# A queue that narrows the float64 weights of the first MLP ahead of their use, and GpSimd for all weight remainders of its first token block

## The chip, the cores and the metric

The kernel runs on one core of one Trainium2 chip. The metric is device time in microseconds (us). The kernel before takes 721.33 us, the median of three runs between 718.95 and 722.62.

## The reference

What is computed is an attention layer with two MLPs behind it, all in float32 accuracy; the weights come as float64.

```python
scores = scale * q @ k.T + bias            # 2 batches, 8 heads, 768 positions, 64 wide
keep = (pos_k < n_global) | (0 <= rel < n_local)
x = softmax(where(keep, scores, -1e9)) @ v # -> 1536 tokens x 512
h = x @ w_in                               # 512 -> 2048
x = (h * cos(h)) @ w_out                   # 2048 -> 512
g = x @ w_gate; val = x @ w_val            # 512 -> 1536, twice
out = (silu(g) * val) @ w_out              # 1536 -> 512
```

## The kernel before, in words

**Tiling.** Tokens go in 12 attention tiles of 128 and in three MLP blocks of 512 (`BLOCKS`). A weight matrix goes in tiles of 128 x 512; the first MLP has 16 of `w1i` and 16 of `w1o`, `NF1` = 16. A float64 weight tile is 512 KB in memory.

**From float64 to two tiles.** `fetch` (L167) loads such a tile into one of the three buffers `st` (L174, on SP's queue). The function that it returns, `narrow`, makes float32 of it on VectorE by three instructions, L183, L186 and L193. The float32 tile `w` stays for the whole kernel. For every use it is split anew: ScalarE makes the rounded main part (L206), and VectorE or GpSimd the remainder (L210). A letter in `WIE` (for `w1i`) and in `WOE` (for `w1o`) says which of the two does the remainder of step n: D for VectorE, G for GpSimd. Every matrix product runs as three TensorE products of main parts and remainders.

**Prologue.** The attention tiles 0 to 3 and the loads for them come first. Its loop (L1007) has 12 windows w. A window issues the scores of one pair of heads' groups (`scores_pair`), the split and the DMA transposes of the window before (`split_p`, L862 and L864), and the products with v two windows later (`pv`, L890). `begin` (L365), called in window 5, fetches `w1i` 0 and 1 and `w1o` 0, narrows the first two and splits the first.

**Steps of the first MLP.** Then come 48 steps s, 16 for each token block (L378 for the first 32). A step has 12 matmuls for h (L274) and 12 for y of two steps before (L350), and a chain of elementwise work for g * cos between them (L300 to L338). In the 16 steps of the first block a step also fetches `w1i` s+2 and `w1o` s+1 (`get`) and, at its end, narrows `w1i` s+2 and `w1o` s (`use`). The attention tiles 4 to 11 are spread over these steps by `BASES`. From step 32 on, and in the second MLP, the order is written out by hand.

**What sets the order.** Until step 32 a planner at compile time orders each engine's instructions from the order in which the code issues them, its own estimates of times, and the buffers; on the chip each engine then runs its list strictly in order. SP's queue is such a list, too: a fetch that waits until a buffer `st` is free holds up the loads of q, k and v and the transposes behind it.

Of the kernel before, what the change touches and what calls it, by code (L numbers as in the profile page):

```python
# [15 lines left out]
I32 = mybir.dt.int32  # L16
# [6 lines left out]
P = 128  # L23
B, H, S, D = 2, 8, 768, 64
NTOK = B * S
DM = H * D
# [19 lines left out]
VSE = "GDDGGGGGGDDD"  # L46
VLE = "DGGGDDDGDDGD"
PLE = "DGGGGGGGDGGGGGGGDGDGGGGGGGGGGDDDDDGDDGDDDDDGDGDG"
WIE = "GGGGGDGGGGGDGGGGDGDGGGDGGDDGDGDGDDDDDDDDDDDDDDDD"
WOE = "GDGDDGDGDDDDGGGGGDDGGGGGGGGDGGGGDDDDDDDDDDDDDDDD"  # L50
SQE = "----DAAAAAAA"
VHE = "DDDDDDDDGDDD"
GKE = "DAAAAADAAAAA"
# [3 lines left out]
VBE = 6  # L57
HB = 5
HE = 6
GVE = "DMMDDDDDDMDM"  # L60
M1E = "GDDGGDG"
ACE = "DDDDDDDD"
# [7 lines left out]
def attention_moe_moe2_kernel(  # L70
# [15 lines left out]
    NF1 = w1i.shape[0]  # L86
# [7 lines left out]
    xy_p = ctx.enter_context(tc.tile_pool(name="xy", bufs=1))  # L94
    wr_p = ctx.enter_context(tc.tile_pool(name="wr", bufs=2 * NF1))
    ws_p = ctx.enter_context(tc.tile_pool(name="ws", bufs=2))
    st_p = ctx.enter_context(tc.tile_pool(name="st", bufs=3))

    n32 = const.tile([P, 2, 2], I32, name="n32")
    for j, src in enumerate((n_global, n_local)):  # L100
# [66 lines left out]
    def fetch(src, j, pool=wr_p, tag="w"):  # L167

        if not wide:
            w = pool.tile([P, DM], F32, tag=tag, name="w")  # L170
            nc.sync.dma_start(out=w, in_=src[j])
            return lambda half=None: w
        t = st_p.tile([P, DM, 2], I32, tag="st", name="st")
        nc.sync.dma_start(out=t, in_=src[j].bitcast(I32).rearrange("p (n w) -> p n w", w=2))  # L174

        part = []

        def narrow(half=None):
            hi, lo = t[:, :, 1], t[:, :, 0]
            if not part:  # L180
                w = pool.tile([P, DM], I32, tag=tag, name="w")
                part.append(w)
                nc.vector.tensor_scalar(  # L183
                    w, hi, 0x07FFFFFF, 3, op0=ALU.bitwise_and, op1=ALU.logical_shift_left
                )
                nc.vector.scalar_tensor_tensor(  # L186
                    out=w, in0=hi, scalar=-(1 << 30), in1=w,
                    op0=ALU.bitwise_and, op1=ALU.bitwise_or,
                )
            w = part[0]  # L190
            if half == 0:
                return None
            nc.vector.scalar_tensor_tensor(  # L193
                out=w, in0=lo, scalar=29, in1=w,
                op0=ALU.logical_shift_right, op1=ALU.bitwise_or,
            )
            return w.bitcast(F32)

        return narrow

    def eng(which, n):
        return nc.vector if n < len(which) and which[n] == "D" else nc.gpsimd
# [20 lines left out]
    def x_split(i, xT):  # L223
        cols = slice(i * P, (i + 1) * P)
        nc.scalar.copy(out=xh[:, :, cols], in_=xT)  # L225
        nc.vector.tensor_tensor(  # L226
            out=xl[:, :, cols], in0=xT, in1=f32(xh[:, :, cols]), op=ALU.subtract
        )
# [16 lines left out]

    def first_mlp(c1, before, steps, last_block):
        w_in, w_out = {}, {}
        got = {}
        todo = [(b, j) for b in range(len(BLOCKS)) for j in range(NF1)]
        nsteps = len(todo)  # L250
        hp = c1.enter_context(tc.tile_pool(name="hp", bufs=2, space=PSUM))
        wis, wos, hps, hs, fs, gs, ys = {}, {}, {}, {}, {}, {}, {}

        def get(nm, j):
            if j < NF1 and (nm, j) not in got:
                got[nm, j] = fetch(w1i if nm == "i" else w1o, j)

        def use(nm, d, j):
            if j < NF1 and j not in d:
                d[j] = got.pop((nm, j))()  # L260

        def prep_in(s):
            if s < nsteps and s not in wis:
# [99 lines left out]
                    )  # L363

        def begin():  # L365
            get("i", 0)
            get("i", 1)
            get("o", 0)
            use("i", w_in, 0)
            use("i", w_in, 1)  # L370
            prep_in(0)

        before(hp, begin, prep_in, h_early)
        ch_p = c1.enter_context(tc.tile_pool(name="ch", bufs=2))
        g_p = c1.enter_context(tc.tile_pool(name="g", bufs=2))
        yp = c1.enter_context(tc.tile_pool(name="yp", bufs=4, space=PSUM))
        last = nsteps - NF1
        for s in range(last):  # L378
            early, late = steps.get(s, ((), ()))
            if s < NF1:  # L380
                get("i", s + 2)
                get("o", s + 1)
            ps = h_mm(s)
            if s >= 2:
                y_mm(s - 2)
            prep_in(s + 1)
            if s >= 1:
                chain_b(s - 1)
            for th in early:
                th()  # L390
            if s >= 1:
                chain_c(s - 1)
                chain_d(s - 1)
            if s < NF1:
                use("i", w_in, s + 2)
                use("o", w_out, s)
            prep_out(s - 1)
            chain_a(s, ps)
            for th in late:
                th()  # L400
# [186 lines left out]
    def windowed_path():  # L587
# [7 lines left out]
        with ExitStack() as ca:  # L595
# [373 lines left out]
                s: tuple([th for _, th in w] for w in e) for s, e in sched.items()  # L969
            }  # L970

            def prologue(hp, begin, prep_in, h_early):
                with (
                    tc.tile_pool(name="pps", bufs=2, space=PSUM, side="right") as pps,
                    tc.tile_pool(name="pv0", bufs=1, side="right") as pv0,
# [31 lines left out]
                    for w in range(NW + LAG + 2):  # L1007
                        if w < NW:
                            i, pp = pairs[w]
# [22 lines left out]
                        if w >= 1 and w - 1 < NW:  # L1032
                            i, pp = pairs[w - 1]
                            for p in (2 * pp, 2 * pp + 1):
                                pools["p"] = (pph, ph_p)[pp]
                                split_p(i, p, eng(PLE, 4 * i + p), nc.scalar.copy)
                        if w == HB:
                            begin()
                        if w == HB + 1:
# [21 lines left out]
    def general_path():  # L1061
        half = TB // 2 * P
        with ExitStack() as cg:
# [19 lines left out]
            for b in range(B):  # L1083
# [6 lines left out]
                for t in range(TB):  # L1090
# [62 lines left out]
                    xn = wk.tile([P, DM], F32, tag="xn", name="gxn")  # L1153
                    nc.vector.tensor_copy(out=xn, in_=x)
                    x_split(i, x_turn(xn, ps_x, "xT"))
        moe(lambda hp, begin, *_: begin(), {}, lambda: None)

    with tc.If(windowed != 0) as branch:
# [45 lines left out]
```

## Time and profile before

| | us |
|---|---|
| median of 3 runs | 721.33 |
| lowest, highest run | 718.95, 722.62 |
| the profiled execution | 719.88 |
| its span, first to last instruction | 718.1 |
| busy in the span: TensorE, VectorE, ScalarE, GpSimd | 668.2, 484.5, 390.0, 112.3 |

All times inside the kernel below come from the profiled execution. PE is TensorE, DVE is VectorE, ACT is ScalarE, POOL is GpSimd, SP the queue that issues the DMAs. The position of a step is read from the count of its matmuls at L274: step 0 ends near 72 us, step 10 starts near 155 us, step 16 near 207 us.

### The profile page before, as it was taken

What the parts mean: (1) busy time and instruction counts of PE and PEld (TensorE: products, weight loads), DVE (VectorE), ACT (ScalarE), POOL (GpSimd) and SP (SyncE); (2) the same over time, 40 slices, a digit from 0 to 9 for tenths busy, and PEclk for the clock granted to TensorE, in tenths of its full rate; (3) what the DMA queues carried; (4) which work ended last, traced back from release to release, by engine and by line L of the source; (5) the groups of instructions that cost most, each with busy time, mean ns of one, the idle gap of its engine ahead of it and who ended that gap; (6) DMA issues with size and microseconds to landing.
All of it is one profiled execution on the core that took longest, in us unless ns stands there. A gap on an engine that the chain in (4) does not pass through costs nothing.

```text
span 718.1 us, 9055 instructions
## 1 busy us (share of the span) xinstructions
PE 668.2 (93%) x3276; PEld 525.9 (73%) x3276; DVE 484.5 (67%) x885; ACT 390.0 (54%) x816; POOL 112.3 (16%) x108
## 2 busy tenths in 40 slices
PE   4767986997998999999999999999999999999996
PEld 2446764775776777787888888888888888888884
DVE  3897899799988565747999779887544443434441
ACT  4675757578497887766666643333343333333331
POOL 2663323423222332420000000000000000000000
PEclk9776899798999999999999999999999999999998
DMA  6799656657552222300322224532100000100001
GB/s 216 184 205 230 166 138 206 137 152 193 147 117 60 40 40 45 60 1 30 112 93 89 88 59 135 158 118 88 38 22 0 1 1 0 59 0 1 1 0 63
DMA packets 69508, 62.73 MB, mean 87 GB/s; under 512 B 48880, under 2 KB 55024, under 8 KB 69456
## 3 DMA queue, kind: packets, MB, share of 16 engines
q1 hardware_dynamic: 69456, 62.08, 31.8%
q8 instruction: 27, 0.44, 0.3%
q14 instruction: 25, 0.20, 0.1%
HBM read 47.19 MB, written 3.15 MB: 70 GB/s over the span
## 4 chain that ended last, share of the span: by engine, by line
PE 77%; DVE 11%; DMA 6%; ACT 3%; issue 1%; POOL 0%; SPq 0%; DVEq 0%; ACTq 0%; POOLq 0%
PE h L274 15%; PE v L492 14%; PE g L492 14%; PE o L528 14%; PE y L350 14%; PE s L753 3%; DMA st<-w1i 2%; DVE w L186 2%; PE x L890 1%; PE s L777 1%; DVE w L193 1%; DMA pt<-ph 1%; DVE w L183 1%; DMA v<-v 1%; DVE h L328 1%
## 5 line engine op out<-in xcount | busy, mean ns | idle before, releaser
L210 DVE TENSOR_TENSOR ws<-w,ws 128x512 fp32r<-128x512 f32 x161 | 111.2, 711 | 93.8 <-ACT ws L206 93.6
L350 PE MATMUL y<-g,ws 128*128 128x512 f32 x576 | 145.1, 397 | 12.6 <-ACT g L332 11.0
L274 PE MATMUL h<-xh,ws 128*128 128x512 f32 (+1 forms) x392 | 137.4, 411 | 2.7 <-ACT xh L225 2.5
L350 PEld LDWEIGHTS y<-g,ws 128*128 128x128 f32 x576 | 108.6, 191 | 39.1 <-ACT g L332 12.9
L206 ACT CAST ws<-w 128x512 fp32r<-128x512 f32 x204 | 121.8, 616 | 21.8 <-DVE w L193 16.8
L528 PE MATMUL o<-ws,a 128*128 128x512 f32 x432 | 104.7, 391 | 0.0
L492 PE MATMUL v<-xh,ws 128*128 128x512 f32 x288 | 96.3, 395 | 0.0
L274 PEld LDWEIGHTS h<-xh,ws 128*128 128x128 f32 x392 | 77.9, 201 | 24.1 <-ACT xh L225 3.2
L492 PE MATMUL g<-xh,ws 128*128 128x512 f32 x288 | 94.7, 390 | 0.0
L528 PEld LDWEIGHTS o<-ws,a 128*128 128x128 f32 x432 | 81.1, 188 | 18.4
L274 PE MATMUL h<-xl,ws 128*128 128x512 f32 (+1 forms) x196 | 79.7, 407 | 3.3 <-DVE xl L226 3.3
L210 POOL TENSOR_TENSOR ws<-w,ws 128x512 fp32r<-128x512 f32 x43 | 58.6, 1363 | 134.6 <-ACT ws L206 126.6
L504 ACT ACTIVATE sl<-g 128x512 f32<-128x512 f32 x36 | 21.5, 598 | 97.5 <-PE g L492 97.5
L492 PEld LDWEIGHTS v<-xh,ws 128*128 128x128 f32 x288 | 54.2, 188 | 12.7
L492 PEld LDWEIGHTS g<-xh,ws 128*128 128x128 f32 x288 | 54.1, 188 | 11.2
L514 ACT CAST a<-sl 128x512 fp32r<-128x512 f32 x36 | 22.4, 623 | 72.5 <-DVE sl L510 72.5
L492 PE MATMUL v<-xl,ws 128*128 128x512 f32 x144 | 56.9, 395 | 0.0
L492 PE MATMUL g<-xl,ws 128*128 128x512 f32 x144 | 56.0, 389 | 0.0
L186 DVE SCALAR_TENSOR_TENSOR w<-st,w 128x512 int32<-128x512 int32 x68 | 51.0, 760 | 1.2
L193 DVE SCALAR_TENSOR_TENSOR w<-st,w 128x512 int32<-128x512 int32 x68 | 50.2, 746 | 0.8
L300 ACT ACTIVATE k<-h 128x512 int32<-128x512 f32 x48 | 28.5, 594 | 39.3 <-PE h L274 39.2
L274 PEld LDWEIGHTS h<-xl,ws 128*128 128x128 f32 x196 | 39.4, 201 | 12.4 <-DVE xl L226 4.0
(109 smaller groups left out, 822.2 us busy)
## 6 DMA issues: line engine op xcount, KB each, us to landing
st<-w1i SPq DMA_DIRECT2D x16, 512.0 KB, 3.9
st<-w1o SPq DMA_DIRECT2D x16, 512.0 KB, 4.4
st<-w2g SPq DMA_DIRECT2D x12, 512.0 KB, 3.8
st<-w2v SPq DMA_DIRECT2D x12, 512.0 KB, 3.7
st<-w2o SPq DMA_DIRECT2D x12, 512.0 KB, 3.8
vr<-v SPq DMA_DIRECT2D x16, 256.0 KB, 3.8
kr<-kT SPq DMA_DIRECT2D x12, 256.0 KB, 3.8
qr<-qT SPq DMA_DIRECT2D x12, 256.0 KB, 3.7
```

The source lines that it names most:

```text
L186: nc.vector.scalar_tensor_tensor(out=w, in0=hi, scalar=-(1 << 30), in1=w, op0=ALU.bitwise_and, op1=ALU.bitwise_or,)
L193: nc.vector.scalar_tensor_tensor(out=w, in0=lo, scalar=29, in1=w, op0=ALU.logical_shift_right, op1=ALU.bitwise_or,)
L206: nc.scalar.copy(out=s[:, 0, :], in_=w)
L210: e.tensor_tensor(out=s[:, 1, :], in0=w, in1=f32(s[:, 0, :]), op=ALU.subtract)
L274: nc.tensor.matmul(hps[s][:, c0:c1], lhsT=wis[s][:, a, k * P:(k + 1) * P], rhs=xx[:, k, t0 + c0:t0 + c1], start=(k == 0 and a == 0 and xx ...
L300: nc.scalar.activation(out=k[:, :n], in_=ps[:, :n], func=AF.Copy, scale=INV2PI)
L350: nc.tensor.matmul(ys[b][m][:, :n], lhsT=w[:, a, m * P:(m + 1) * P], rhs=g[:, c, :n], start=(j == 0 and a == 0 and c == 0), stop=(j == NF1 ...
L492: nc.tensor.matmul(ps[:, :n], lhsT=w[:, a, k * P:(k + 1) * P], rhs=xx[:, k, t0:t0 + n], start=(k == 0 and a == 0 and xx is xh), stop=(k == ...
L504: nc.scalar.activation(out=sl[:, :n], in_=ps_.pop(("g", s))[:, :n], func=AF.Silu)
L514: nc.scalar.copy(out=a[:, 0, :n], in_=sl[:, :n])
L528: nc.tensor.matmul(os_[b][m], lhsT=a[:, c, m * P:(m + 1) * P], rhs=w[:, d, :], start=(j == 0 and c == 0 and d == 0), stop=(j == NF2 - 1 an ...
L753: nc.tensor.matmul(o, lhsT=qr[r, i % 3, c, :], rhs=k, start=True, stop=True)
```

## The change

It does two things. First, the fetches and the narrowing of the first MLP's 32 weight tiles no longer follow the steps. A list `order` holds them in the order of use; `fetch_next` fetches the next one; `conv1` narrows the oldest one fetched and fetches the next. Three fetches are issued at the very start, ahead of the branch and so ahead of the loads of k, q and v for the tiles 1 and on. In the prologue's windows `conv1` is called `CV[w]` times, 13 times in all in the windows 0 to 10; each step of the first block calls it twice, and `need(s)` calls it more often only where a tile would be missing. The three buffers `st` become one tile with three slots, used in turn. Second, ten letters D in the first 16 places of `WIE` and `WOE` become G: 5 and 11 in `WIE`; 1, 3, 4, 6, 8, 9, 10 and 11 in `WOE`.

```diff
-WIE = "GGGGGDGGGGGDGGGGDGDGGGDGGDDGDGDGDDDDDDDDDDDDDDDD"
-WOE = "GDGDDGDGDDDDGGGGGDDGGGGGGGGDGGGGDDDDDDDDDDDDDDDD"
+WIE = "GGGGGGGGGGGGGGGGDGDGGGDGGDDGDGDGDDDDDDDDDDDDDDDD"
+WOE = "GGGGGGGGGGGGGGGGGDDGGGGGGGGDGGGGDDDDDDDDDDDDDDDD"
+CV = (2, 2, 1, 1, 1, 1, 1, 1, 1, 1, 1)
...
-    st_p = ctx.enter_context(tc.tile_pool(name="st", bufs=3))
+    st_p = ctx.enter_context(tc.tile_pool(name="st", bufs=1))
+    st = st_p.tile([P, 3, DM, 2], I32, name="st")
+    taken = [0]
...
-        t = st_p.tile([P, DM, 2], I32, tag="st", name="st")
+        t = st[:, taken[0] % 3]
+        taken[0] += 1
...
+    order = [t for j in range(NF1 + 2) for t in (("i", j), ("o", j - 2)) if 0 <= t[1] < NF1]
+    fetched = []
+    def fetch_next():
+        if order:
+            nm, j = order.pop(0)
+            fetched.append(((nm, j), fetch(w1i if nm == "i" else w1o, j)))
+    for _ in range(3):
+        fetch_next()
...
+        def conv1():
+            if fetched:
+                (nm, j), fn = fetched.pop(0)
+                (w_in if nm == "i" else w_out)[j] = fn()
+                fetch_next()
+        def need(s):
+            while (s + 2 < NF1 and s + 2 not in w_in) or (s < NF1 and s not in w_out):
+                conv1()
...
         def begin():
-            get("i", 0)
-            get("i", 1)
-            get("o", 0)
-            use("i", w_in, 0)
-            use("i", w_in, 1)
+            while 1 not in w_in:
+                conv1()
             prep_in(0)
...
             if s < NF1:
-                get("i", s + 2)
-                get("o", s + 1)
...
             if s < NF1:
-                use("i", w_in, s + 2)
-                use("o", w_out, s)
+                conv1()
+                conv1()
+                need(s)
...
+                        for _ in range(CV[w] if w < len(CV) else 0):
+                            conv1()
                         if w == HB:
                             begin()
```

## Rows read from the trace of the kernel before

**Rows 1.** The page's part 2: busy tenths in 40 slices of 18 us.

```profile
PE   4767986997998999999999999999999999999996
DVE  3897899799988565747999779887544443434441
```

**Rows 2.** Busy time by stretch: PE, PEld, DVE, ACT, POOL, granted clock, DMA share, GB/s.

```profile
12.00:72.00 60.00, 43.24 (x305) 27.85 (x305) 44.06 (x74) 38.22 (x120) 28.67 (x24) 0.77 0.88 222
72.00:155.00 83.00, 73.04 (x359) 54.24 (x359) 73.36 (x151) 57.07 (x124) 29.13 (x22) 0.88 0.61 166
155.00:207.00 52.00, 47.47 (x252) 36.03 (x251) 49.69 (x103) 36.32 (x85) 14.39 (x12) 0.93 0.59 162
207.00:330.00 123.00, 121.03 (x686) 94.26 (x685) 78.60 (x161) 96.55 (x198) 36.19 (x28) 1.00 0.21 38
```

**Rows 3.** The chain that ended last: start us, us, what.

```profile
7.46 5.53 DMA v<-v
22.18 4.94 DMA vr<-v
...
61.41 3.58 DMA pt<-ph
...
104.73 3.96 DMA st<-w1i
108.69 0.02 issue
108.72 0.76 DVE w L183 x2
```

**Rows 4.** The prologue's first loads: two SP issues, then two stretches (columns of Rows 2).

```profile
2.39 0.60 SPq L115 DMA_DIRECT2D qr<-qT  x1
6.20 0.56 SPq L110 DMA_DIRECT2D kr<-kT  x1
...
8.00:12.00 4.00, 1.97 (x11) 1.26 (x10) 2.94 (x10) 1.22 (x4) 1.50 (x2) 1.00 0.86 268
12.00:20.00 8.00, 5.71 (x17) 2.69 (x19) 1.03 (x4) 5.88 (x23) 0.01 (x1) 1.00 0.75 280
```

**Rows 5.** The narrowing's lines in 12 to 72 us (first three) and 155 to 207 us.

```profile
L186 DVE SCALAR_TENSOR_TENSOR w<-st,w 128x512 int32<-128x512 int32 x5 | 3.4, 682 | 0.0
L193 DVE SCALAR_TENSOR_TENSOR w<-st,w 128x512 int32<-128x512 int32 x4 | 2.7, 684 | 0.0
L183 DVE TENSOR_SCALAR w<-st 128x512 int32<-128x512 int32 x6 | 2.4, 417 | 0.0
...
L193 DVE SCALAR_TENSOR_TENSOR w<-st,w 128x512 int32<-128x512 int32 x10 | 8.6, 872 | 0.0
L186 DVE SCALAR_TENSOR_TENSOR w<-st,w 128x512 int32<-128x512 int32 x10 | 7.7, 782 | 0.0
L183 DVE TENSOR_SCALAR w<-st 128x512 int32<-128x512 int32 x10 | 7.1, 753 | 0.3 <-DMA st<-w1i 0.3
```

**Rows 6.** DVE in order of time, its two longest gaps before 72 us.

```profile
18.09 0.17 DVE L897 TENSOR_SCALAR r<-sum 128x8 f32<-128x8 f32 x1 [6.28 <-ACT sb L809]
...
65.81 0.41 DVE L736 COPY vs<-relt 32x1024 f16<-32x1024 f16 x1 [3.26 <-PE x L890]
```

**Rows 7.** DVE's waits from 72 to 207 us: total us, times, longest us.

```profile
DVE sb L829 <- PE s L753: 6.5, 6, 3.2
DVE w L183 <- DMA st<-w1i: 2.0, 4, 0.8
```

**Rows 8.** The remainders: POOL's in 72 to 207 us, DVE's in 155 to 207 us.

```profile
L210 POOL TENSOR_TENSOR ws<-w,ws 128x512 fp32r<-128x512 f32 x18 | 25.7, 1433 | 71.3 <-ACT ws L206 64.1 <-DVE w L183 7.2
...
L210 DVE TENSOR_TENSOR ws<-w,ws 128x512 fp32r<-128x512 f32 x4 | 2.7, 681 | 0.0
```

**Rows 9.** One meeting of POOL and DVE, in order of time.

```profile
119.74 2.96 POOL L862 TENSOR_TENSOR ph<-sb,ph 128x512 f16<-128x512 f32 x2
...
120.26 1.11 DVE L897 TENSOR_SCALAR r<-sum 128x8 f32<-128x8 f32 x1
```

**Rows 10.** Waits from 72 to 207 us: SP's longest, and TensorE's longest.

```profile
SPq L174 <- DVE w L193: 47.0, 21, 5.0
...
PE y L350 <- ACT g L332: 10.8, 4, 5.7
```

More of the change, by code (lines that the diff above doesn't have):

```diff
@@ L199, in fetch @@
         return narrow
+    order = [t for j in range(NF1 + 2) for t in (("i", j), ("o", j - 2)) if 0 <= t[1] < NF1]
+    every = list(order)
+    fetched = []
[5 more added lines that the diff above has]
+        fetch_next()
     def eng(which, n):
@@ L247, in first_mlp @@
         w_in, w_out = {}, {}
-        got = {}
         todo = [(b, j) for b in range(len(BLOCKS)) for j in range(NF1)]
@@ L252, in first_mlp @@
         wis, wos, hps, hs, fs, gs, ys = {}, {}, {}, {}, {}, {}, {}
[L254 to L260, printed above, removed]
+        def conv1():
[6 more added lines that the diff above has]
+                conv1()
         def prep_in(s):
@@ L365, in begin @@
         def begin():
-            get("i", 0)
-            get("i", 1)
-            get("o", 0)
-            use("i", w_in, 0)
-            use("i", w_in, 1)
+            while 1 not in w_in:
+                conv1()
             prep_in(0)
-        before(hp, begin, prep_in, h_early)
+        before(hp, begin, prep_in, h_early, conv1)
         ch_p = c1.enter_context(tc.tile_pool(name="ch", bufs=2))
@@ L379, in first_mlp @@
             early, late = steps.get(s, ((), ()))
-            if s < NF1:
-                get("i", s + 2)
-                get("o", s + 1)
             ps = h_mm(s)
@@ L970, in windowed_path, with prologue @@
             }
-            def prologue(hp, begin, prep_in, h_early):
+            def prologue(hp, begin, prep_in, h_early, conv1):
                 with (
@@ L1155, in general_path @@
                     x_split(i, x_turn(xn, ps_x, "xT"))
+        del fetched[:]
+        order[:] = every
+        for _ in range(3):
+            fetch_next()
         moe(lambda hp, begin, *_: begin(), {}, lambda: None)
```

## The prediction, made before the kernel ran

> **What bounds the kernel now.** I read the page's slices first, then the chain of waits, then busy time by stretch. The slices [rows 1] show two kernels in one: from the thirteenth slice on (216 us) TensorE is at nine tenths or more almost throughout, before that VectorE is the fuller engine. The stretches [rows 2] give the numbers. From 207 to 330 us TensorE is busy 121.03 of 123 us at the full granted clock, so nothing that the change does can be worth more there than 2 us, and I take 0. All that can move lies ahead of 207 us, in three stretches:
> - the prologue (12 to 72 us): VectorE 44.06 of 60 us, DMA share 0.88, TensorE 43.24 at a clock of 0.77;
> - steps 0 to 9 (72 to 155): VectorE 73.36 of 83, TensorE 73.04 at 0.88;
> - steps 10 to 15 (155 to 207): VectorE 49.69 of 52, TensorE 47.47 at 0.93.
>
> The chain [rows 3] runs in the prologue over the loads of v and a transpose, and in the steps over VectorE, with fetches between: at 104.73 a fetch of `w1i` takes 3.96 us and VectorE's narrowing stands right behind it. That looks like a DMA bound, but the table of VectorE's waits [rows 7] says otherwise: the narrowing waited for a fetch only 2.0 us in all, four times. VectorE had other work while the DMA ran; it is bound by its amount of work. TensorE's own long wait, 10.8 us for ACT's g [rows 10], is behind VectorE's queue.
>
> So the question is one of VectorE's time: the change removes hardly any of its work. It moves narrowing from the steps 10 to 15, where TensorE would soon be the next limit, into the prologue, where VectorE and the DMA engines are nearly full.
>
> **Part 1: three fetches at the very start.** SP has issued q at 2.39 and issues k again only at 6.20 [rows 4], because the branch lies between. The three fetches (3 x 524 KB = 1.57 MB) go into this gap. At the 268 to 280 GB/s that the next stretches moved [rows 4] they take 5.7 us; some 3.2 us of that fall where the DMA engines had nothing to do. The rest, 2.5 us, delays the loads of k, q and v behind them on the same queue, and the load of v is on the chain [rows 3]. Bounds: 0 (all hidden) to 5.7 us; I take 2.5.
>
> **Part 2: narrowing in the prologue.** A narrowing costs 0.417 + 0.682 + 0.684 = 1.78 us in the prologue and 0.753 + 0.782 + 0.872 = 2.41 us in the steps 10 to 15 [rows 5]. Before, 4 tiles are narrowed by 72 us (the count of L193); after, 13, so nine more: 16 us at 1.78, 22 at 2.41. VectorE is idle 60 - 44.06 = 15.9 us there [rows 2]. The longest hole is 6.28 us up to 18.09, the next 3.26 us up to 65.81 [rows 6]. The first takes three tiles (their data are there by then; the 3 us that the three earliest narrowings took later come free), the second nearly two, the many holes under 1.2 us perhaps 2.5 us of work. About 12 us of the 16 to 18 hide, which leaves +5. The delay of part 1 opens a hole of its own, in which narrowing fits, so the two don't add up: +6 for the prologue together, bounds +1 (nearly all hidden) and +13 (rival 2). Who pays: each `conv1` also puts a fetch on SP's queue that waits until VectorE has narrowed the slot; queued behind it are the transposes for `pv` and the loads. Such waits are normal in the steps (47.0 us in 21 waits [rows 10]) and hurt little there; `pv` comes two windows after its transposes, which covers one narrowing of 1.8 us, but at the prologue's end, where a transpose of 3.58 us is on the chain [rows 3], it isn't covered. That is in the +6.
>
> **Part 3: steps 0 to 9.** Two calls a step narrow the other 19 tiles here. Before, 18 were narrowed in this stretch: one more, +2.2 (between 1.78 and 2.41, nearer to the second, since GpSimd is at work here too). The fetch now runs three narrowings ahead, a step and a half, so the waits for fetches go: -1.7 of the 2.0. Some of VectorE's other 8 us of idle time (6.5 us of waits for scores over both stretches [rows 7]) should fill, as the queued tiles are work that waits for nothing: -0.6. Bounds for this filling: 0 and -5.
>
> **Part 4: ten remainders to GpSimd,** six of them in steps 0 to 9, four in steps 10 to 12. Each takes 0.68 us from VectorE and costs GpSimd 1.43 us [rows 8]; GpSimd is busy 29.13 of 83 us [rows 2], so six times 1.43 fit, and a remainder is needed only a step later. But it isn't free for VectorE. At 120.26 a VectorE instruction on 8 elements took 1.11 us while GpSimd ran [rows 9]; the same instruction alone takes 0.17 [rows 6]. On average less: narrowing in 155 to 207 us is 0.63 us dearer a tile than in the prologue [rows 5], 6.3 us for 10 tiles, beside 12 instructions of GpSimd [rows 2]: 0.53 us for each. So the six save 6 x (0.68 - 0.53) = 0.9 us, bounds -4.1 (no stall) and +1.6 (0.94 us each). Steps 0 to 9 come to +2.2 - 1.7 - 0.6 - 0.9 = -1.
>
> The Trainium skill speaks against this part. "SBUF — State Buffer", section "Who interferes with whom", says that a VectorE instruction with two SBUF inputs and a GpSimd instruction that reads SBUF exclude each other for the whole instruction, and the later one blocks fully. The trace agrees in the direction (the 0.94 us above), not in the average.
>
> **Part 5: steps 10 to 15.** No narrowing is left: VectorE's 49.69 us lose 23.4 [rows 5] and it is no longer the limit. TensorE is next: 47.47 us busy, of which the clock of 0.93 (part of the stretch at the lower level, 1.2 GHz) accounts for 0.07 x 52 = 3.6. So 43.9 to 47.5 us in place of 52; I take 45.5, -6.5. ACT, with 36.32 us, stays below that.
>
> **Sum.** +6 - 1 - 6.5 + 0 = -1.5 on the profiled execution's 719.88 us: 718.4. That execution was 1.45 us under the median of 721.33, so I predict 720 us.
>
> **The rivals.**
> 1. *VectorE's holes fill well.* Queued tiles are always ready, so idle time falls everywhere: prologue +1.5, steps 0 to 9 -4, steps 10 to 15 down to TensorE's 43.9 us (-8): -10.5, some 711 us; with half of it, 715. For it: 25.6 us of VectorE idle ahead of 155 us [rows 2]. Against it: an engine runs its list in order, and a list made at compile time hits holes of under 1 us only by luck.
> 2. *The prologue becomes DMA-bound: slower.* By 72 us nine more fetches are issued than before; at 1.9 us each (0.524 MB at 280 GB/s [rows 4]) that is 17 us of the DMA engines. The gap at the start gives 3, the idle share (0.12 x 60) 7. The other 7, with 2 for transposes behind fetches at the end (a fetch of 1.9 us ahead of each of the last) and 4 of narrowing that the holes don't take, make the prologue 13 us longer. Steps as above: 13 - 7.5 = +5.5, some 727 us. It decides from a prologue that is 11 us longer. For it: DMA share 0.88 [rows 2] and two DMA pieces of 5 us on the chain [rows 3]. Against it: the last fetches may land during step 0 without harm.
> 3. *GpSimd blocks VectorE for each whole instruction.* Then the six cost 6 x (1.43 - 0.53) = 5.4 us more than in the sum: 725 us. For it: the single meeting in [rows 9]. Against it: the mean of 0.53. The Trainium skill's page named above would give this.
> 4. *The change doesn't do what it says.* The planner may put the added narrowing late in each queue, since nothing needs it soon; then the stretches stay as they are, 721 us.
>
> **How the numbers follow.** About 0.5%, 3.6 us, is what a measurement of this kernel can tell from no change. Chances: my forecast 0.32, rival 1 0.34, rival 2 0.22, rival 3 0.06, rival 4 0.06. That makes 0.38 for within 0.5%, 0.34 for faster and 0.28 for slower. The likeliest group is the one around no change, and its time is 720 us, with 718 to 724 as its own range. The cases on both sides hold more than half of the chance, so the range reaches to both: 711 to 729.
>
> **What would show it.** In the profile after: two or three narrowings before 18 us; step 0 ending near 78 us rather than 72; in the next stretch 19 narrowings and no wait for `st`; six steps in some 45 us with VectorE near half busy; TensorE's full stretch beginning within 2 us of 207. If step 0 ends at 74 or earlier, rival 1 has it; at 83 or later, rival 2. If VectorE's narrowing or its small instructions are much dearer than 2.2 us and 0.17 in the steps, rival 3. The prediction is wrong altogether if the planner orders the prologue in a new way, so that the 43 us of TensorE's work there move against the rest, which none of the rows can tell.

## The result and the profile after

The changed kernel takes 727.11 us, the median of seven runs between 725.08 and 729.57; the kernel before, beside it, took 720.41. The ratio is 1.0097, with a 95% interval from 1.0075 to 1.0118: slower by 1%, where the prediction said no change. Here and below a ratio compares all comparable runs on the same chip, so it is not exactly the quotient of the medians.

The profiled execution took 726.1 us, with a span of 724.3; before it was 719.88 and 718.1. So 6.2 us are to be found.

First the page's slices, as in [rows 1], and the granted clock under them:

```profile
PE   3594799789999999999999999999999999999996
DVE  6899899773648575647998868887543444434441
PEclk9757699697999999999999999999999999999998
```

VectorE is fuller in the first slices and emptier from the ninth to the twelfth. TensorE is emptier in the first slices, and from the ninth to the thirteenth on the whole a little fuller. The prologue and the time behind the first token block in numbers (columns of [rows 2]):

```profile
12.00:72.00 60.00, 37.56 (x259) 21.96 (x260) 52.55 (x93) 36.38 (x115) 29.49 (x24) 0.74 0.96 241
207.00:330.00 123.00, 121.65 (x688) 94.74 (x687) 75.24 (x161) 98.21 (x209) 36.71 (x29) 1.00 0.22 42
```

Against [rows 2]: in the prologue VectorE has 52.55 us in place of 44.06, and TensorE gets through 37.56 us of work in place of 43.24.

**Where the 6.2 us are.** A step is marked by the first of its 12 matmuls for h, the same one in both traces. Step 1 begins at 80.5 us (before 71.7), step 10 at 167.0 (154.7), step 16 at 212.8 (207.0). Steps 0 to 9 before and after (from the start of step 1, as in [rows 2]), and then steps 10 to 15 before and after:

```profile
71.69:154.67 82.98, 73.02 (x359) 54.06 (x359) 73.17 (x150) 56.74 (x123) 29.13 (x22) 0.88 0.61 167
80.48:166.99 86.51, 75.59 (x361) 55.94 (x361) 74.01 (x156) 62.79 (x135) 43.88 (x34) 0.86 0.66 181
154.67:207.02 52.35, 47.82 (x254) 36.33 (x254) 49.89 (x104) 36.67 (x86) 14.39 (x12) 0.93 0.60 162
166.99:212.81 45.82, 44.45 (x245) 34.23 (x245) 25.16 (x60) 33.32 (x76) 12.77 (x10) 0.96 0.22 53
```

The prologue lost 8.8 us, steps 0 to 9 lost 3.5, steps 10 to 15 gave back 6.5, and behind them 0.4 were lost: 8.8 + 3.5 - 6.5 + 0.4 = 6.2. In steps 10 to 15 VectorE's load fell from 49.89 to 25.16 us, near the 26.3 that were forecast, and TensorE was busy for 44.45 of the 45.82 us. The DMA share fell from 0.60 to 0.22: the fetches are over.

The planner moves some work across the steps, so I also add up TensorE's matmuls in both traces, each at its shortest duration in the trace of before, and compare when the same sum is reached ("equal work"). The delay of after is then 1.8 us near 17 us, 8.8 at the prologue's end (71.0 against 79.8), 6.9 where before stands at 143.8, 13.4 at 159, 7.5 at 205.4, and 6.3 to 6.4 from 225 on. It rises and falls with single waits of TensorE: after has one ahead of its step 10 (2.45 us, at 160.56), before has two behind its step 10 (1.90 and 2.60 us, at 171.62 and 174.88) that after no longer has.

Such positions come from one execution of each kernel. Eight of the kernels below have the prologue of before, with the same list for TensorE, VectorE and SP; in them step 1 begins at 70.1 to 73.8 us. A difference of 2 us there says nothing.

**The start.** SP's first issues (start us, us, queue and line, tiles; before's in [rows 4]):

```profile
2.38 0.60 SPq L118 DMA_DIRECT2D qr<-qT  x1
3.03 0.43 SPq L178 DMA_DIRECT2D st<-w1i  x1
6.18 0.81 SPq L178 DMA_DIRECT2D st<-w1i  x2
7.14 0.57 SPq L113 DMA_DIRECT2D kr<-kT  x1
```

Only the first of the three fetches goes into the gap; SP issues the other two behind it, at 6.18 and 6.56, and k starts at 7.14, before at 6.20. In the code the three stand behind the load of the branch's flag (`values_load`), and the planner drew one ahead of it. So the sentence on the change that all three are issued ahead of the branch is not what the chip did. VectorE's list, in the same form, has the second narrowing between the maxima of the scores:

```profile
12.57 0.41 DVE L187 TENSOR_SCALAR w<-st 128x512 int32<-128x512 int32 x1
13.51 0.68 DVE L190 SCALAR_TENSOR_TENSOR w<-st,w 128x512 int32<-128x512 int32 x1
14.31 0.68 DVE L197 SCALAR_TENSOR_TENSOR w<-st,w 128x512 int32<-128x512 int32 x1
```

Three tiles are narrowed by 16.8 us.

**The prologue's end.** The chain that ended last (start us, us, what; before's in [rows 3]):

```profile
66.46 0.71 PE xT L237 x3
67.17 3.98 DMA vs<-relt
...
71.20 2.41 PE x L905 x42
...
73.63 1.38 DVE vs L751
75.01 0.61 DVE xn L918
...
77.46 3.44 PE h L294 x13
```

Before, the same h (13 matmuls of 3.44 us, the chain's last of the prologue) started at 68.67. The last small transfer for the global positions (`vs` from `relt`) was issued at 58.92 before, at 67.17 after.

**The steps.** The waits of 72 to 207 us (columns of [rows 10]):

```profile
PE y L370 <- ACT g L352: 7.1, 2, 6.1
PE s L768 <- DVE mx L844: 2.5, 1, 2.5
...
DVE w L187 <- DMA st<-w1i: 0.8, 2, 0.5
```

The narrowing in 72 to 155 us (columns of [rows 5]):

```profile
L190 DVE SCALAR_TENSOR_TENSOR w<-st,w 128x512 int32<-128x512 int32 x20 | 18.1, 917 | 0.1
L197 DVE SCALAR_TENSOR_TENSOR w<-st,w 128x512 int32<-128x512 int32 x20 | 17.1, 864 | 0.0
L187 DVE TENSOR_SCALAR w<-st 128x512 int32<-128x512 int32 x19 | 10.5, 564 | 0.8 <-DMA st<-w1i 0.8
```

All 32 tiles are narrowed by 150 us, before by 202. The waits for fetches fell from 2.0 us to 0.8. What is left for TensorE is few single waits. The chain ahead of the longest:

```profile
120.25 4.28 DMA st<-w1i
...
124.56 0.92 DVE w L187
125.48 3.23 DVE w L190 x2
...
130.19 0.69 DVE h L348
...
130.90 0.59 ACT g L352
...
131.54 2.08 PE y L370 x4
```

VectorE narrows a tile here that is needed only steps later, and the h that ScalarE and TensorE want stands behind it in VectorE's list. Of what stands ahead of h the wait for the fetch is the smallest part, 0.50 us (in brackets the wait, and what ended it):

```profile
124.56 0.92 DVE L187 TENSOR_SCALAR w<-st 128x512 int32<-128x512 int32 x1 [0.50 <-DMA st<-w1i]
```

The rest is the narrowing, and its two instructions at 125.48 are dear: 3.23 us for two that take 0.68 each alone. GpSimd was at work beside them (start us, us):

```profile
122.79 3.81 POOL L227 TENSOR_TENSOR ws<-w,ws 128x512 fp32r<-128x512 f32 x2 [9.29 <-ACT ws L223]
126.70 3.01 POOL L877 TENSOR_TENSOR ph<-sb,ph 128x512 f16<-128x512 f32 x2
```

After the wait TensorE runs at the lower level, 1.2 GHz (stretches, columns of [rows 2]; the last but two is the granted clock):

```profile
131.00:134.00 3.00, 2.46 (x6) 1.62 (x7) 2.92 (x8) 3.00 (x7) 1.92 (x2) 0.50 0.94 219
134.00:138.00 4.00, 4.00 (x13) 2.83 (x12) 2.70 (x8) 2.67 (x7) 2.97 (x3) 0.50 1.05 290
138.00:142.00 4.00, 4.00 (x11) 3.00 (x11) 2.24 (x6) 0.33 (x1) 1.67 (x2) 0.50 0.70 136
142.00:146.00 4.00, 4.00 (x17) 2.95 (x16) 3.29 (x7) 2.69 (x6) 2.24 (x2) 0.83 0.00 1
```

Before has the same kind of wait, 5.67 us at 124.98, and there too a narrowing, at 115 to 120 us, stands ahead of the h in VectorE's list. Ahead of the second wait, 2.45 us at 160.56, VectorE's split of v stood still 2.81 us for a cast on GpSimd that had a remainder ahead of it:

```profile
158.67 1.14 DVE L735 TENSOR_TENSOR vs<-vr,vs 128x512 f16<-128x512 f32 x1 [2.81 <-POOL vs L734]
```

### The profile page after: what moved, and what is told of

Same layout as the page of the kernel before. It is cut to its first block, busy times and chain, and to the rows that moved or that the text cites. A ratio compares the mean times of both kernels' runs of the same rounds, so it can differ in the third digit from the quotient of the medians.

```text
span 724.3 us, 9060 instructions
## 1 busy us (share of the span) xinstructions
PE 669.0 (92%) x3276; PEld 526.2 (73%) x3276; DVE 475.1 (66%) x875; ACT 392.4 (54%) x818; POOL 128.0 (18%) x118
## 4 chain that ended last, share of the span: by engine, by line
PE 76%; DVE 13%; ACT 5%; DMA 3%; issue 1%; POOL 1%; SPq 0%; ACTq 0%; POOLq 0%; DVEq 0%
PE v L507 14%; PE y L370 14%; PE g L507 14%; PE o L543 13%; PE h L294 13%; PE s L768 3%; DVE w L190 2%; DVE w L197 2%; PE x L905 2%; PE s L792 2%; DVE w L187 1%; DMA st<-w1i 1%; DMA pt<-ph 1%; DVE h L348 1%; ACT sb L862 1%
## 5 line engine op out<-in xcount | busy, mean ns | idle before, releaser
L227 DVE TENSOR_TENSOR ws<-w,ws 128x512 fp32r<-128x512 f32 x151 | 103.0, 705 | 93.8 <-ACT ws L223 93.7
L294 PE MATMUL h<-xh,ws 128*128 128x512 f32 (+1 forms) x392 | 134.7, 405 | 2.3 <-ACT xh L242 1.4
L223 ACT CAST ws<-w 128x512 fp32r<-128x512 f32 x204 | 121.8, 615 | 16.3 <-DVE w L197 10.4
L227 POOL TENSOR_TENSOR ws<-w,ws 128x512 fp32r<-128x512 f32 x53 | 73.1, 1381 | 131.6 <-ACT ws L223 131.5
L294 PEld LDWEIGHTS h<-xh,ws 128*128 128x128 f32 x392 | 75.8, 196 | 23.9 <-issue 3.4
L294 PE MATMUL h<-xl,ws 128*128 128x512 f32 (+1 forms) x196 | 78.2, 399 | 2.0 <-DVE xl L243 2.0
L507 PEld LDWEIGHTS g<-xh,ws 128*128 128x128 f32 x288 | 54.1, 188 | 11.2
L190 DVE SCALAR_TENSOR_TENSOR w<-st,w 128x512 int32<-128x512 int32 x68 | 51.9, 767 | 1.4
L197 DVE SCALAR_TENSOR_TENSOR w<-st,w 128x512 int32<-128x512 int32 x68 | 52.1, 768 | 0.9
L348 DVE SCALAR_TENSOR_TENSOR h<-f,h 128x512 f32<-128x512 f32 x48 | 33.2, 692 | 24.1 <-ACT f L341 23.9
L320 ACT ACTIVATE k<-h 128x512 int32<-128x512 f32 x48 | 28.5, 594 | 35.2 <-PE h L294 35.0
```

The costliest lines, as they stand in the source:

```text
L190: nc.vector.scalar_tensor_tensor(out=w, in0=hi, scalar=-(1 << 30), in1=w, op0=ALU.bitwise_and, op1=ALU.bitwise_or,)
L197: nc.vector.scalar_tensor_tensor(out=w, in0=lo, scalar=29, in1=w, op0=ALU.logical_shift_right, op1=ALU.bitwise_or,)
L223: nc.scalar.copy(out=s[:, 0, :], in_=w)
L227: e.tensor_tensor(out=s[:, 1, :], in0=w, in1=f32(s[:, 0, :]), op=ALU.subtract)
L294: nc.tensor.matmul(hps[s][:, c0:c1], lhsT=wis[s][:, a, k * P:(k + 1) * P], rhs=xx[:, k, t0 + c0:t0 + c1], start=(k == 0 and a == 0 and xx ...
L320: nc.scalar.activation(out=k[:, :n], in_=ps[:, :n], func=AF.Copy, scale=INV2PI)
```

## The experiments

Two theories for the slower time. *P*: the queue lengthens the prologue, and the steps can't give that back, since they are held by single waits and not by VectorE's load. *G*: the ten letters are what costs, by GpSimd. Each part alone first.

**The queue alone (`queue_only`)**: the kernel after, with the letters of before.

```diff
-WIE = "GGGGGGGGGGGGGGGGDGDG...
-WOE = "GGGGGGGGGGGGGGGGGDDG...
+WIE = "GGGGGDGGGGGDGGGGDGDG...
+WOE = "GDGDDGDGDDDDGGGGGDDG...
```

> The changed kernel with the letters of before: the queue alone. Theory P (the prologue: nine more narrowings and fetches ahead of step 0 cost some 8.6 us and the steps can't give them back): as slow as the change, 725 to 729 us, step 0 ending near 80 us. Theory G (the ten remainders on GpSimd hold up VectorE's and GpSimd's lists, as at 158 us of the changed kernel, and eat what the queue gains in the steps): back to 718 to 722 us, step 0 still ending near 80 us but the delay gone by step 16.

728.38 us, ratio 1.011 (1.0076 to 1.0144). The queue alone costs what the whole change costs.

**The letters alone (`letters_only`)**: the kernel before, with the letters of after.

> The kernel before with the ten letters of the change, without the queue. Theory P: no difference, 719 to 722 us, since each remainder saves VectorE 0.68 us and costs it about 0.53. Theory G: slower by 3 to 6 us, 723 to 727 us.

725.91 us, ratio 1.0097 (1.0062 to 1.0133). The letters alone cost as much again. The two prices don't add up: together they are 1.0097. Step 1 begins at 70.7 us here and at 82.1 with the queue alone (read from the longest of its six executions): the letters' price lies in the steps, the greater part of the queue's ahead of them.

**The queue's two halves.** `cv_none` keeps the early fetches and calls `conv1` in no window; `late_fetch` keeps the windows and issues the first three fetches behind the prologue's loads of v.

```diff
-CV = (2, 2, 1, 1, 1, 1, 1, 1, 1, 1, 1)
+CV = ()
```

> The changed kernel with an empty CV: three fetches still at the very start and the queue in use, but no narrowing in the windows beyond the two that the first split needs; the steps narrow two tiles each as before. Theory P: the prologue is short again (step 0 ends at 72 to 75 us) and the time goes back to 718 to 722 us. Theory S (the start: the three early fetches delay q, k and v and with them the prologue): step 0 ends at 75 us or later, 723 us or more.

729.51 us, ratio 1.0142 (1.0102 to 1.0182).

```diff
-    for _ in range(3):
-        fetch_next()
...
+                    for _ in range(3):
+                        fetch_next()
                     for w in range(NW + LAG + 2):
```

> The changed kernel with its first three fetches issued behind the loads of k, q and v of the prologue rather than ahead of the branch. Theory S: the prologue gets 2 to 3 us shorter, some 724 us. Theory P: those fetches only move into the stretch where the DMA engines and VectorE are full, so no gain: 726 to 729 us.

731.22 us, ratio 1.0163 (1.0134 to 1.0192). Neither half alone is better. `queue_inert` takes both away, with the letters of before: the queue then only feeds the steps.

> The queue of the change with the letters of before, an empty CV, and the first three fetches behind the prologue's loads: the queue without running ahead. Theory P with S (what costs is the early start and the narrowing ahead, not the queue): 719 to 723 us, step 0 ending at 71 to 74 us. If the queue as such costs (its fetches wait on VectorE in SP's list ahead of transposes): 725 us or more.

722.53 us, ratio 1.0035 (1.001 to 1.006). The four kernels make a square. "Delay" is that at equal TensorE work where before stands at 71.0 us:

| | fetches at the start | fetches behind v |
|---|---|---|
| `conv1` in the windows | after: +8.8, ratio 1.0097 | `late_fetch`: +13.3, 1.0163 |
| none in the windows | `cv_none`: +6.7, 1.0142 | `queue_inert`: 0.0, 1.0035 |

(`queue_inert` has the letters of before, the others those of after; by `letters_only` these do nothing to the prologue, so the delays can be compared, but not the ratio of `queue_inert` with the other three.) This is theory P for the prologue: with both halves of the queue out of it, it is as long as before. And the early start, which alone costs 6.7 us, saves some 3 to 4.5 once the windows narrow (`queue_only`, with the prologue of after, has +10.4).

**What makes the prologue long: VectorE's time, or the transfers?** `one_op` gives a tile of the first 13 one instruction in place of three; `small_fetch` loads 64 of 512 columns of the fetches 4 to 16; `both` does both.

```diff
                 nc.vector.tensor_scalar(
                     w, hi, 0x07FFFFFF, 3, op0=ALU.bitwise_and, op1=ALU.logical_shift_left
                 )
+                if n < 13:
+                    return w.bitcast(F32)
```

> The changed kernel in which the first 13 tiles, those called for in the prologue, are narrowed by one instruction in place of three (two of the three are left out, so these weights are wrong): VectorE's share of the prologue's loss. 13 x 1.36 = 18 us of VectorE's work less there. If VectorE's work makes the prologue long: step 0 ends at 72 to 75 us and the whole takes 717 to 722 us. If it is the transfers: step 0 still ends at 78 us or later, 724 us or more.

730.33 us, ratio 1.0153 (1.0131 to 1.0174), and step 1 begins at 79.4 us (read from an execution of 721.91 us, the shortest of five).

```diff
+        n = taken[0]
...
-        nc.sync.dma_start(out=t, in_=src[j].bitcast(I32).rearrange("p (n w) -> p n w", w=2))
+        c = slice(0, 64 if 3 <= n < 16 else DM)
+        nc.sync.dma_start(out=t[:, c, :], in_=src[j].bitcast(I32).rearrange("p (n w) -> p n w", w=2)[:, c, :])
```

> The changed kernel in which the 13 fetches after the first three move 64 KB in place of 512 KB (the rest of the tile is what the slot held before, so these weights are wrong): the DMA share of the prologue's loss. If the transfers make it long: step 0 ends at 72 to 75 us, 717 to 722 us. If it is VectorE's work: step 0 ends at 78 us or later, 724 us or more.

727.15 us, ratio 1.0098 (1.0075 to 1.0121), and step 1 begins at 80.4 us. The prologue's stretch, `one_op` first (columns of [rows 2]):

```profile
12.00:72.00 60.00, 39.65 (x268) 24.05 (x269) 37.61 (x70) 35.95 (x115) 28.05 (x24) 0.81 0.95 244
```

And `small_fetch`:

```profile
12.00:72.00 60.00, 39.18 (x276) 24.41 (x276) 50.56 (x88) 37.44 (x118) 31.22 (x26) 0.80 0.72 182
```

With VectorE's 37.61 us, less than before's 44.06, the prologue is as long as after's; with a DMA share of 0.72, less than before's 0.88, it is as long, too. Neither amount is the bound by itself.

> The changed kernel with both reliefs of the prologue at once: the first 13 tiles narrowed by one instruction in place of three, and the 13 fetches after the first three cut to 64 KB (these weights are wrong). Theory Q (two limits stand side by side in the prologue, VectorE's list and the DMA side, so that easing either alone leaves the other): step 0 ends at 72 to 75 us, the whole at 718 to 722 us. If it still ends at 78 us or later, neither the narrowing's nor the transfers' amount makes the prologue long, but the order of the lists.

723.8 us, ratio 1.0056 (1.003 to 1.0082); step 1 begins at 76.8 us (read from an execution of 730.48 us, the longest of seven). With both amounts cut, hardly anything is left of the delay in the prologue's middle (0.7 us where before stands at 56.0), and 5.1 of the 8.8 us at its end. That speaks for two limits side by side, which carry some 3.7 us together; what is left at the end is neither. With 2 us of scatter in the start of step 1 the shares are rough.

**Is it SP's list?** After 39.65 us SP issues without a gap in the kernel after until some 72 us. From its list, 59.88 us and on (start us, us):

```profile
59.88 0.36 SPq L178 DMA_DIRECT2D st<-w1o  x1
...
61.74 4.70 SPq L879 DMA_TRANSPOSE pt<-ph  x2
66.54 0.54 SPq L178 DMA_DIRECT2D st<-w1i  x1
67.17 0.58 SPq L749 DMA_DIRECT2D vs<-relt  x1
```

The transfer of 67.17 that stands on the chain waits behind these. `fetch_pool` and `fetch_act` put the fetches on the queues of GpSimd and of ScalarE, those of the second MLP too (from step 32 on both take as long as before, within 1 us).

```diff
-        nc.sync.dma_start(out=t, in_=src[j].bitcast(I32)...
+        nc.gpsimd.dma_start(out=t, in_=src[j].bitcast(I32)...
```

> The kernel after, with the fetches of the weights issued from GpSimd's queue and no longer from SP's. The amounts of transfers and of VectorE's work stay the same; SP's list loses the fetches and their waits, and is free for the transposes and loads. If SP's list is what makes the prologue long, step 0 ends at 72 to 75 us and the whole takes 719 to 722 us. If it is the amount of work for VectorE and the DMA engines, step 0 ends at 79 to 81 us, as in the kernel after, and the whole takes 726 to 729 us. A fetch that waits for its buffer now holds up GpSimd's remainders and casts behind it, which can cost some us in the steps by itself; so the end of step 0 decides, not the whole.

732.81 us, ratio 1.0185 (1.0143 to 1.0227), and step 1 begins at 80.5 us, although SP's list has gaps now:

```profile
60.16 3.19 SPq L879 DMA_TRANSPOSE pt<-ph  x2
66.40 0.57 SPq L749 DMA_DIRECT2D vs<-relt  x1
67.11 2.79 SPq L879 DMA_TRANSPOSE pt<-ph  x2
```

SP is through with its transposes at 63.35 and waits until 66.40 for what it is to issue. So the prologue is as long without a full SP list, which was the story that I would have told from the trace of after alone. What this doesn't clear are the fetches' waits for a slot: they stand in GpSimd's list now, ahead of the casts that the transposes wait for. GpSimd's longest wait from 12 to 80 us (total us, times, longest us):

```profile
POOL st L178 <- DVE w L197: 12.8, 6, 4.5
```

> The same with the fetches on ScalarE's queue. SP's list: step 0 ends at 72 to 75 us. Amount of work: 79 to 81 us. Here a fetch that waits for its buffer holds up ScalarE, which has the exponentials of the prologue and the g of the steps behind it, so the whole may well be slower than the kernel after (727 to 735 us) under either theory.

755.63 us, ratio 1.0509 (1.0456 to 1.0562); step 1 begins at 104.0 us. ScalarE, held up by fetches that wait for a buffer, makes the prologue 24 us longer still. This tells of ScalarE's place in the prologue, not of SP.

**Does an earlier v help by itself?** `early_v` puts into the gap at the start not the weights but the loads of k, q and the first v, with the letters and narrowings of before.

```diff
+    load_k(1)
+    load_q(1)
+    v0 = []
+    for u in range(2):
...
+        nc.sync.dma_start(
+            out=vv, in_=v[2 * u * P:(2 * u + 2) * P, :].rearrange("(t p) c -> p t c", p=P)
+        )
```

> The kernel before with k and q of tile 1 and the first four tiles of v loaded ahead of the branch, where the change put three weight fetches (v goes through two of the buffers st, so the fetch of w1o 0 comes a little later). The load of v is on the chain of waits: if the gap ahead of the branch is worth something, it is worth it there. Expected: the first v tile lands 3 to 5 us earlier, step 0 ends at 67 to 70 us, the whole takes 715 to 718 us. If VectorE holds the prologue anyway: 719 to 722 us.

724.03 us, ratio 1.0049 (1.0028 to 1.0069). The prologue's middle is 4.0 us earlier than before (where before stands at 56.0), its end 0.8 (equal work): what is won early in the prologue is gone by its end. So its end is not set by the chain of v from its beginning.

**The letters.** Is it the order (any new order costs), the one cast on GpSimd, or the count? `swap_a` keeps the counts and moves every D among the first 16 letters of `WOE` one place later and both of `WIE` one earlier; `swap_b` changes only two neighbours in `WOE`.

```diff
-WOE = "GDGDDGDGDDDDGGGGGDDG...
+WOE = "GGDDDGDGDDDDGGGGGDDG...
```

> The kernel before with the same number of letters D at other places: in WIE 4 and 10 in place of 5 and 11; in WOE each of the eight moved on by one place. VectorE's and GpSimd's work is the same to the instruction, only the planner's order from step 1 on differs. Theory N (the letters of before go with an order that happens to be good, and any other order costs some us): 723 to 728 us, as with the ten letters gone. Theory G (it is the work on GpSimd that costs): no difference, 719 to 722 us.

718.55 us, ratio 0.9982 (0.9961 to 1.0003).

> The kernel before with one letter D of WOE moved from place 1 to place 2 and nothing else. Theory N: slower by 2 us or more, 723 to 728 us. Theory G: 719 to 722 us.

716.28 us, ratio 0.9962 (0.9939 to 0.9985).

> The kernel of swap_b once more (2 becomes D and 1 becomes G in WOE, nothing else changed), for the size of its gain: it took 0.9962 of the time of before in ten runs. If the gain is one of the order of the instructions it comes back, 0.994 to 0.998 of before; if it was the scatter of the runs, 0.999 to 1.001.

717.54 us, ratio 0.9975 (0.9958 to 0.9992). So not every new order costs: these two don't, and one exchange of two letters gains 0.38% and 0.25%. It is the fastest kernel here. Of the orders that the planner makes of four, six or ten more letters G this says nothing.

`vhe_d` has the ten letters and gives GpSimd's cast of v (the one that the wait of 2.81 us was for) to VectorE.

```diff
-VHE = "DDDDDDDDGDDD"
+VHE = "DDDDDDDDDDDD"
```

> The kernel before with the ten letters of the change, and the one cast of v's main part that GpSimd does (tile 8) given to VectorE. Theory L (a remainder on GpSimd costs by standing in GpSimd's list ahead of that cast, for which VectorE waits in order, and TensorE for VectorE, as at 146 to 154 us of the run with the letters alone): most of the 5 us come back, 719 to 722 us. If the price is the sum of VectorE's stalls beside GpSimd: still 724 to 727 us.

727.83 us, ratio 1.0109 (1.0076 to 1.0143): not that cast alone. Then the ten in two groups, and six letters the other way.

```diff
-WIE = "GGGGGDGGGGGDGGGG...
-WOE = "GDGDDGDGDDDDGGGG...
+WIE = "GGGGGGGGGGGDGGGG...
+WOE = "GGGGGGGGGDDDGGGG...
```

> The kernel before, with only six of the ten letters turned to GpSimd: 5 in WIE and 1, 3, 4, 6, 8 in WOE (steps 0 to 9). All ten alone cost some 5 us (725.9 against 720.8). If every remainder moved to GpSimd costs its share (0.5 us each), six cost 3 us: 722.5 to 723.5. If the price is made at one place, by one or two GpSimd operations that someone waits for, this kernel carries all of it (724.5 to 726) or none (719 to 721). My prediction's own term for these six was -0.9.

727.43 us, ratio 1.0108 (1.0051 to 1.0165).

> The kernel before, with only the other four letters turned to GpSimd: 11 in WIE and 9, 10, 11 in WOE (steps 9 to 12). Share for share: 4 x 0.5 = 2 us, 721.5 to 722.5. If the price is made at one place, all of it (724.5 to 726) or none (719 to 721), the opposite of the run with the six.

722.35 us, ratio 1.0061 (1.0042 to 1.008).

```diff
+WIE = "GGGDGDGGDGGDGDGG...
+WOE = "GDDDDDDDDDDDGGGG...
```

> The kernel before, with six letters turned the other way, from GpSimd to VectorE: 3, 8, 13 in WIE and 2, 5, 7 in WOE. All ten of the change, six of them alone and the other four alone each made the kernel slower by 0.6 to 1.1%. If GpSimd's remainders are too dear in themselves (each stalls VectorE, or comes late), the opposite step is faster: 714 to 717 us. If before stands at a balance, so that every shift of work between the two engines costs, it is slower too: 722 to 727 us, by VectorE's 6 x 0.68 = 4.1 us of added work.

720.32 us, ratio 1.001 (0.9988 to 1.0032). Both groups cost, and together no more than the six alone. The three intervals just allow one price for each letter, some 0.1%: 0.62 to 1.33% for ten, 0.51 to 1.65% for six, 0.42 to 0.80% for four. But at that price `more_d`, six letters the other way, should be 0.6% faster, and it isn't. The other theory, a balance, would have made it slower by 0.3% or more. Both failed. VectorE's whole busy time in `more_d`, from the page:

```profile
PE 674.2 (93%) x3276; PEld 530.2 (73%) x3276; DVE 480.8 (67%) x891; ACT 392.5 (54%) x818; POOL 103.4 (14%) x102
```

It has six instructions more than before, 4.1 us at 0.68, and its sum is 480.8 us, before's 484.5. In `swap_a` and `swap_b`, with the counts of before, it is 477.3 and 479.6. So it varies by 7 us at equal work, with how VectorE's and GpSimd's instructions happen to meet. A few remainders more or less are below that. It also means that `more_d` did not make VectorE fuller, so it is no test of whether VectorE's load is the bound.

## Why the prediction was wrong, point by point

The time lies in the range (711 to 729), but the forecast, no change, is wrong: it is slower by 1%. By stages:

| us | forecast | measured |
|---|---|---|
| prologue (parts 1 and 2) | +6 | +8.8 |
| steps 0 to 9 (parts 3 and 4) | -1 | +3.5 |
| steps 10 to 15 (part 5) | -6.5 | -6.5 |
| behind them | 0 | +0.4 |
| sum | -1.5 | +6.2 |

**What bounds the kernel.** The step that failed is "VectorE is bound by its amount of work", applied to steps 0 to 9: there the sum of parts 3 and 4 counts VectorE's work and lets its idle time fill. The work came nearly as forecast, the idle time did not (parts 3 and 4 below). Between kernels the length of these steps doesn't go with VectorE's work either. `queue_inert` and then `swap_b`, from the start of step 1 to that of step 10 (columns of [rows 2]):

```profile
71.66:159.18 87.52, 78.87 (x361) 57.53 (x360) 69.85 (x153) 59.42 (x130) 30.21 (x23) 0.83 0.60 160
72.20:152.90 80.70, 71.94 (x360) 53.20 (x359) 72.72 (x151) 56.49 (x123) 28.67 (x22) 0.90 0.64 174
```

With less work for VectorE (69.85 us against 72.72) and the same number of matmuls, the steps took 6.8 us more. What goes along with the length is TensorE's granted clock, 0.83 against 0.90: TensorE ran at the lower level for longer.

**Part 1** (+2.5 for v): the first product with v's data came at 15.50 us in place of 13.69, +1.8. But the mechanism is in part another. Two of the three fetches did not go into the gap; they hold up k by 0.94 us on SP's list, which the sum lacked, and the transfers ran faster than the 280 GB/s assumed. That the term came near is in part luck. From 12 to 20 us:

```profile
12.00:20.00 8.00, 3.90 (x12) 1.66 (x12) 4.83 (x12) 5.22 (x21) 0.03 (x1) 1.00 1.06 390
```

**Part 2** (prologue +6): +8.8 at equal work and by the start of step 1, within the bounds; step 0 was to end near 78 us and ended at 80.7. Direction and place were right, the size short by 2.8. Up to step 1 VectorE got 59.96 - 44.06 = 15.9 us more work, as forecast; 7.1 us of it fell into its idle time (15.6 us before, 8.5 after), where I had 12. A narrowing cost 0.620 + 0.738 + 0.848 = 2.21 us in 12 to 72 us, not 1.78 (first to last line by the lines below), and 12 were done by 72 us, not 13. But the picture, work that doesn't fit into VectorE's holes, is not what the runs show: `one_op` took two thirds of it out and the prologue stayed.

```profile
L187 DVE TENSOR_SCALAR w<-st 128x512 int32<-128x512 int32 x12 | 7.4, 620 | 1.3 <-DMA st<-w1i 1.3
L190 DVE SCALAR_TENSOR_TENSOR w<-st,w 128x512 int32<-128x512 int32 x12 | 8.9, 738 | 0.1
L197 DVE SCALAR_TENSOR_TENSOR w<-st,w 128x512 int32<-128x512 int32 x12 | 10.2, 848 | 0.1
```

**Parts 3 and 4** (-1 for steps 0 to 9) came to +3.5, read from one execution each; `swap_a` and `swap_b`, with the counts of before, have 80.7 to 81.4 us there against before's 83.0. In their own terms: VectorE's work was to grow by 2.2 - 0.9 = 1.3 us and grew by 74.01 - 73.17 = 0.8. Its idle time was to fall by 1.7 + 0.6 = 2.3 us and grew by 2.7, from 82.98 - 73.17 = 9.8 to 86.51 - 74.01 = 12.5. The waits for fetches did fall (2.0 to 0.8 us up to 207 us), but other waits came; the longest is that of 2.81 us for GpSimd's cast. TensorE waited behind it for 2.45 us and then ran at the lower level. So the filling of idle time by queued work is what failed. For the six letters I took -0.9, bounds -4.1 and +1.6; alone on the kernel before they cost 1.08% (interval 0.51 to 1.65), outside the bounds. Beside the queue letters cost nothing more (1.011 without, 1.0097 with). To price a remainder by VectorE's time alone was wrong: the tile also comes by another list, at another time.

**Part 5** (-6.5 for steps 10 to 15) came true: 45.82 us, where I took 45.5, with VectorE at 25.16 us and TensorE busy for 44.45. "VectorE is no longer the limit" and "TensorE is next" hold here, and the other kernels bear it out. In the eight that narrow in the windows these steps take 44.8 to 49.1 us, in the eleven that narrow in the steps, before among them, 51.3 to 54.1 (`cv_none`, which only fetches early, 49.4). That it fits so closely is luck, since the border is: after's wait at 160.56 and the lower level behind it lie just ahead of step 10. Parts 3 to 5 together had -7.5 and came to -3.0.

With the measured sizes the sum is 8.8 + 3.5 - 6.5 + 0.4 = +6.2, where I had +6 - 1 - 6.5.

**The rivals.** Rival 2 gave 727 us, the time that came, but for another reason: a prologue 13 us longer by transfers, with 7.5 us given back; measured are 8.8 and 3.0. `small_fetch` cut the transfers and the prologue stayed. Rival 1 (holes fill) didn't come: it had steps 0 to 9 4 us shorter, and VectorE's idle time there grew. Rival 3 (GpSimd blocks for each whole instruction): the meeting at 125.48 shows 0.94 us more for each of two VectorE instructions, (3.23 - 2 x 0.68) / 2, and GpSimd's were longer too, 1.9 us each in place of the 1.43 of [rows 8]. The Trainium skill's "SBUF — State Buffer", section "Who interferes with whom", has the later of the two blocked fully; this meeting agrees: three VectorE instructions with two inputs, one after the other, end at 127.15, 128.70 and 130.27 us, each some 0.55 us after a GpSimd instruction ends (126.60, 128.15 and 129.71). The row at 120.26 in [rows 9], on which the prediction rested this, is an instruction with one input tensor. That the blocking makes the letters' price isn't shown: VectorE's sums differ by more at equal work. Rival 4 didn't come: narrowings stand from 8 us on.

**What stays open.** Which order of waits makes the prologue long: VectorE's amount, the transfers and a full list of SP don't do it, each alone, and both amounts together are some two fifths of it; the fetches' waits for a slot, in whichever list they stand, are not excluded. And by which waits the letters cost 0.6 to 1.1% alone: excluded are that every new order costs, that one cast, and a price that each letter has either way; that the orders which the planner makes of them are bad ones is not excluded. To take single waits out of the lists was not tried.

## What to carry to other kernels

Ask of each stage what a change adds to an engine's work and what it adds to its idle time; the second does not follow from the first. In steps 10 to 15 VectorE's work was the bound: taking half of it away made them 6.5 us shorter. In steps 0 to 9, with VectorE 88% busy, its work stayed and they became 3.5 us longer by waits. Work that is queued ahead is not free filling: in an engine's list, run in order, it puts its own time and the wait for its DMA into the path of whoever is behind it. Moving work from a later stretch into an earlier one pays only if the later one gives back more than the earlier one loses, here 6.5 against 8.8. To see it, mark a step by the same matmul in both traces, and check it at equal work of the bound engine.

## What the runs showed of the hardware that I had not expected

- The issue of one fetch of 512 KB held SP for 0.33 to 0.67 us, that of one DMA transpose for 1.2 to 2.9 us (12 of them in the kernel after from 39.65 to 71 us).
- Loads in parallel reached 390 GB/s from 12 to 20 us, where before 280 were moved.
- Two VectorE instructions of 0.68 us took 3.23 us together beside GpSimd, and GpSimd's two 3.81 us in place of 2.9; each of the VectorE instructions ended some 0.55 us after a GpSimd instruction.
- After a wait of 6.11 us TensorE's granted clock was 0.50 for some 11 us, although it was busy throughout from 134 us on.
- The same fetches from GpSimd's queue made the kernel after slower by 732.81 - 727.11 = 5.7 us, from ScalarE's by 28.5 (medians from different chips, so rough). The wait for a free slot then stands in that engine's list.
